# First batch of a fused attention and FFN kernel: k's first heads over a hardware queue, q in token quarters, units of scores formed as their data lands, v in three pieces

## The chip, the cores and the metric

One core of a Trainium2 chip; the runs are spread over several chips. The metric is the device time of one execution in microseconds (us). The profiled span is about 1.75 us shorter than the time of the same execution, and 1 us is 0.17% of it, so this case is about tenths of a per cent.

## The reference

Linear attention with keys and values projected from 1024 to 64 positions, then a SwiGLU FFN. Cut to what matters:

```python
# q, k, v: (8 batches, 8 heads, 1024 tokens, 64); E, F: (64, 1024)
k_proj = einsum('ks,bhsd->bhkd', E, k)
v_proj = einsum('ks,bhsd->bhkd', F, v)
scores = (q @ k_proj.transpose(0, 1, 3, 2)) / 8
attn = softmax(scores)                       # over 64 positions
x = (attn @ v_proj) -> (8192 tokens, 512)    # heads side by side
g = x @ w_gate                               # 512 x 1536
out = (silu(g) * (x @ w_val)) @ w_out
```

## The kernel before

Everything runs in bf16 on TensorE; GpSimd's loads cast fp32 to bf16 on the way. The attention of batch b+1 is woven into the FFN of batch b. Only the first batch has nothing to hide behind, and the change concerns it alone. Its work is written as units, called in the order in which TensorE runs them:

- `turn`: E or F to bf16 and token-major (fp32 transposes on TensorE, then a copy).
- `u_KV`: k or v of some heads times E or F, then casts out of PSUM (`ks` for k; `BDV` for v).
- `u_KT`: ks transposed into the block-diagonal `BD` (four copies by VectorE).
- For each of four units u of the first token half (u = 2 x head group + token pair): `u_T` transposes q, `u_S` forms scores and exp (ACT), `u_R` row sums and reciprocals (VectorE), `u_N` the product `AA` (GpSimd or VectorE), `u_A` transposes AA into `AT`.
- `u_PV2`: AT times BDV gives `xT`, which `f_mm` multiplies by the FFN's weights.
- `warm`: matmuls on zeros that keep TensorE busy. `load_w_gv(a, b)`: the columns of f = a to b-1 of w_gate and w_val.
- The first token half is 512 tokens. The first FFN groups take them as two parts of 256; where "second token half" is said of an FFN group, the second 256 are meant.

```python
# loads are issued in this order by GpSimd; E and F by SP
load_k(0, 0, 4)
... E, F ...
load_k(0, 4, 8)
load_q(0, 0, 2)            # first token half of q, as two groups of heads
load_v(0, (0, 4, 8))       # v as two halves
load_w_gv(0, 1); load_w_gv(1, 2); load_w_gv(2, 4)
warm(8); turn(0); turn(1); warm(7)
u_KV(0, "k", (0, 4), at="y")
...                        # u_KT, then k's second half, u_KT
...                        # u_T and u_S of the four units, u_R, u_N of units 0 and 2
load_w_gv(4, 6, (0,))
u_KV(0, "v", (0, 4), at="y")
...                        # A0, products of units 1 and 3, A2
u_KV(0, "v", (4, 8), at="y")
...                        # the other loads; u_PV2, A1, A3, and four half groups of f_mm
```

The softmax here doesn't subtract the row's maximum and nothing guards it: scores larger than these inputs give would overflow.

Of the kernel before, what the change touches and what calls it, by code (L numbers as in the profile page):

```python
# [12 lines left out]
BF16 = mybir.dt.bfloat16  # L13
FP32 = mybir.dt.float32

B = 8
H = 8
S = 1024
D = 64
KP = 64  # L20
DM = H * D
DFF = 1536
P = 128
NJ = S // P
# [10 lines left out]
def kernel(  # L35
# [19 lines left out]
    nc = tc.nc  # L55
# [4 lines left out]
    kv_pool = ctx.enter_context(tc.tile_pool(name="kv", bufs=2))  # L60
# [22 lines left out]
    kb, vb, qb, xT, hT = {}, {}, {}, {}, {}  # L83

    def load_k(b, h0=0, h1=H):
        if h0 == 0:
            kb[b] = kv_pool.tile([P, H, NJ, D], BF16, name="kb", tag="kb")
        nc.gpsimd.dma_start(  # L88
            out=kb[b][:, h0:h1].rearrange("p h j d -> p h (j d)"),
            in_=k[b, h0:h1].rearrange("h (p j) d -> p h (j d)", j=NJ),  # L90
        )

    def load_v(b, heads=(0, H)):
        t = kv_pool.tile([P, H, NJ, D], BF16, name="vb", tag="vb")
        vb[b] = t
        for h0, h1 in zip(heads, heads[1:]):
            nc.gpsimd.dma_start(
                out=t[:, h0:h1].rearrange("p h j d -> p h (j d)"),
                in_=v[b, h0:h1].rearrange("h (p j) d -> p h (j d)", j=NJ),
            )  # L100

    def load_q(b, ch, parts=1):
        t = q_pool.tile([P, H, 4, D], BF16, name="qb", tag="qb")
        qb[b, ch] = t
        n = H // parts
        for i in range(parts):
            nc.gpsimd.dma_start(  # L107
                out=t[:, i * n : (i + 1) * n].rearrange("p h j d -> p h (j d)"),
                in_=q[b, i * n : (i + 1) * n].rearrange("h (p c j) d -> p c h (j d)", c=2, j=4)[:, ch],
            )  # L110

    def load_w_gv(c0, c1, which=(0, 1)):
        cs = slice(c0 * P, c1 * P)
        for wsrc, wdst in [((moe_w_gate, wg), (moe_w_val, wv))[i] for i in which]:
            nc.gpsimd.dma_start(
                out=wdst[:, :, cs],
                in_=wsrc[:, cs].rearrange("(t p) c -> p t c", p=P),
            )
# [11 lines left out]
    def bank(where, shape, dt, name):  # L130
        pool, tag = banks[where]
        return pool.tile(shape, dt, name=name, tag=tag)

    def copy(eng, out, in_):
        (nc.scalar.copy if eng is nc.scalar else eng.tensor_copy)(out=out, in_=in_)  # L135
# [31 lines left out]
    def u_KT(b, at="a", prs=(0, NPAIR)):  # L167

        ks = kvp[b, "s"]
        t = bank(at, [P, NPAIR, KP], BF16, "kTp")  # L170
        for pr in range(*prs):
            nc.tensor.transpose(  # L172
                out=t[:, pr, :],
                in_=ks[:, 2 * pr : 2 * pr + 2, :].rearrange("p h d -> p (h d)"),
                identity=ident_bf[:KP, :KP],
            )
        bd = BD[b % 2][:].rearrange("p (a c) k -> p a c k", c=2)
        for c in range(2):
            src = t[64 * c : 64 * c + 64, slice(*prs)]
            nc.vector.tensor_copy(out=bd[0:64, slice(*prs), c, 0:64], in_=src)  # L180
            nc.vector.tensor_copy(out=bd[64:128, slice(*prs), c, 64:128], in_=src)
# [65 lines left out]
    def u_N(b, u):  # L247
        ch, w = divmod(u, 4)
        g, i = divmod(w, 2)
        if (b, ch) in BY_DMA:  # L250
            if (b, ch, "d") not in AA:
                AA[b, ch, "d"] = aw.tile([P, 4, H, KP], BF16, name="AAd", tag="AAd")
            a = AA[b, ch, "d"][:, 2 * i : 2 * i + 2, 4 * g : 4 * g + 4, :]
        else:
            a = AA[b, u] = aw.tile([P, 2, 4, KP], BF16, name="AA", tag="AA", bufs=4)
            a = a[:]
        eng = nc.vector if b == 0 and u in (2, 3) else nc.gpsimd
        eng.tensor_tensor(  # L258
            out=a.rearrange("p j h k -> p h j k"),
            in0=ee.pop((b, u))[:],  # L260
            in1=rr.pop((b, u))[:].unsqueeze(3).to_broadcast([P, 4, 2, KP]),
            op=ALU.mult,
        )
# [160 lines left out]
            fn(*a)  # L424

    with tc.manual_schedule():
        load_k(0, 0, 4)
        ef = []
        for which, src in (("E", E), ("F", F)):
            raw = const.tile([KP, S], FP32, name=f"{which}raw")  # L430
# [7 lines left out]
            nc.vector.memset(BD[i][:], 0.0)  # L438
            nc.vector.memset(BDV[i][:], 0.0)

        def turn(which):
            for half in range(2):
                ps = bank("v", [P, 4, KP], FP32, "efp")
                for i in range(4):
                    j = 4 * half + i
                    nc.tensor.transpose(
                        out=ps[:, i, :],
                        in_=ef[which][:, bass.ds(j, P, step=NJ)],
                        identity=ident_fp[:KP, :KP],
                    )  # L450
                js = slice(4 * half, 4 * half + 4)
                copy((nc.scalar, nc.vector)[which], (ET, FT)[which][:, js, :], ps[:])

        def warm(n):

            ps = bank("v", [P, CW], FP32, "warm")
            for _ in range(n):
                nc.tensor.matmul(
                    out=ps[:], lhsT=zeros[:, 0:P], rhs=zeros[:],
                    start=True, stop=True,  # L460
                )


        load_k(0, 4, 8)
        load_q(0, 0, 2)
        load_v(0, (0, 4, 8))
        load_w_gv(0, 1)
        load_w_gv(1, 2)
        load_w_gv(2, 4)
        warm(8)  # L470
        turn(0)
        turn(1)
        warm(7)
        u_KV(0, "k", (0, 4), at="y")
        warm(2)
        u_KT(0, at="v", prs=(0, 2))
        warm(2)
        u_KV(0, "k", (4, 8), at="y")
        warm(2)
        u_KT(0, at="v", prs=(2, 4))  # L480
        u_T(0, 0, "a", nc.scalar)
        u_T(0, 1, "a", nc.vector)
        u_T(0, 2, "a", nc.scalar)
        u_S(0, 0, "g")
        u_T(0, 3, "v", nc.vector)
        u_S(0, 2, "g")
        u_S(0, 1, "a")
        u_S(0, 3, "a")
        u_R(0, 0)
        u_N(0, 0)  # L490
        u_R(0, 2)
        u_N(0, 2)
        load_w_gv(4, 6, (0,))
        u_KV(0, "v", (0, 4), at="y")
        warm(1)
        u_A(0, 0, nc.scalar)
        u_R(0, 1)
        u_N(0, 1)
        u_R(0, 3)
        u_N(0, 3)  # L500
        u_A(0, 2, nc.scalar)
        u_KV(0, "v", (4, 8), at="y")
        load_w_gv(4, 6, (1,))
        load_q(0, 1)
        load_w_gv(6, 8)
        load_w_gv(8, 10)
        load_w_gv(10, 12)
        load_wo(0)
        load_wo(1)
        load_k(1)  # L510
        warm(1)
        u_PV2(0, 0, 0, 0, nc.scalar)
        u_PV2(0, 0, 1, 0, nc.vector)
        u_A(0, 1, nc.scalar)
        u_A(0, 3, nc.vector)
        f_mm(0, 0, 0, 0)
        f_mm(0, 0, 1, 0)
        u_PV2(0, 0, 0, 1, nc.scalar)
        u_PV2(0, 0, 1, 1, nc.vector)
        f_mm(0, 1, 0, 0)  # L520
        f_mm(0, 1, 1, 0)

# [32 lines left out]
        for t in range(NIT):  # L555
            c, f = divmod(t, NFT)
# [40 lines left out]
```

## Time and profile before

| | before |
|---|---|
| time, median of 3 | 574.07 us (573.66 to 574.24) |
| span of the profiled run | 572.4 us |
| k's first heads land; their matmuls start | 9.70; 9.74 |
| k's other heads land; their matmuls start | 12.25; 12.29 |
| v's last byte lands; v's last matmuls start | 20.01; 20.05 |
| marker: first f=0 group of the second token half | 24.88 |
| from marker to end | 547.5 |

Read it from the bottom: 547.5 us of TensorE work without a gap follow the marker, so a change to the opening can win only by moving the marker (24.88). Each step above the marker starts 0.04 us after its data lands. Windows of the profile before: after the window and its length, busy time of PE, PEld, DVE, ACT and POOL with counts; then the granted clock, a DMA figure that is not used here, and GB/s.

```profile
20.00:23.00 3.00, 2.70 (x23) 1.98 (x25) 2.53 (x6) 1.97 (x5) 2.82 (x4) 1.00 1.64 189
23.00:26.00 3.00, 3.00 (x29) 2.68 (x29) 0.89 (x2) 1.07 (x2) 2.93 (x5) 1.00 1.45 196
```

After v, the weights stream on at the same pace, 189 and 196 GB/s (the last column).

### The profile page before, as it was taken

The numbers are of one execution on the slowest core, as the hardware profiler recorded it, in microseconds if no ns is written. First come the engines' busy times: TensorE is split into PE (matmuls) and PEld (weight loads), VectorE is DVE, ScalarE is ACT, GpSimd is POOL, SyncE is SP. The second block draws the span as 40 slices with busy tenths as digits, with TensorE's granted clock in tenths as the row PEclk, the third lists the DMA queues.
The fourth block names the chain that finished last, engine by engine and source line by source line (L and its number), as shares of the span: only waits on it lengthen the run. The fifth ranks groups of instructions, "written<-read, shape, count | busy, mean of one in ns | idle before, by whom it ended". The sixth has DMA issues, their size and how long they took to land.

```text
span 572.4 us, 7867 instructions
## 1 busy us (share of the span) xinstructions
PE 561.2 (98%) x2910; PEld 268.6 (47%) x2967; DVE 336.8 (59%) x580; ACT 237.0 (41%) x416; POOL 107.9 (19%) x121
## 2 busy tenths in 40 slices
PE   8899999999999999999999999999999999999997
PEld 4654544444444444444444444444444444444444
DVE  2787566666466744766556665567546674554550
ACT  1655444353425434444335434354342543443232
POOL 6734131234002400124001330023200220000000
PEclk9999999999999999999999999999999999999999
DMA  9999993539901698037951399204990124100012
GB/s 160 196 200 206 201 161 74 93 64 196 201 37 41 110 190 157 18 75 129 187 108 38 59 179 195 63 22 88 197 176 37 42 52 74 38 37 25 31 39 92
DMA packets 105927, 61.34 MB, mean 107 GB/s; under 512 B 58016, under 2 KB 97696, under 8 KB 105888
## 3 DMA queue, kind: packets, MB, share of 16 engines
q0 software_dynamic: 42288, 29.89, 36.1%
q1 hardware_dynamic: 63312, 30.68, 25.1%
q8 instruction: 23, 0.38, 0.3%
q10 hardware_dynamic: 288, 0.26, 0.1%
q14 instruction: 16, 0.13, 0.1%
HBM read 60.29 MB, written 16.78 MB: 135 GB/s over the span
## 4 chain that ended last, share of the span: by engine, by line
PE 94%; DMA 2%; POOL 1%; ACT 1%; issue 1%; DVE 0%; POOLq 0%
PE yps L360 29%; PE vps L322 29%; PE gps L322 29%; PE kvp L147 3%; PE sc L227 2%; DMA vb<-in_v_dram 2%; PE pv L285 2%; PE aTp L274 0%; ACT xT L135 0%; PE qTp L193 0%; POOL kb L88 0%; PE kTp L172 0%; POOL qb L107 0%; ACT th L334 0%; PE pv L300 0%
## 5 line engine op out<-in xcount | busy, mean ns | idle before, releaser
L341 DVE SCALAR_TENSOR_TENSOR s<-th,gps 128x512 f32<-128x512 f32 x192 | 130.5, 680 | 138.0 <-ACT th L334 137.8
L322 PE MATMUL gps<-xT,wg 128*128 128x512 bf16 (+1 forms) x755 | 195.7, 377 | 1.2
L322 PE MATMUL vps<-xT,wv 128*128 128x512 bf16 (+1 forms) x761 | 195.9, 377 | 0.8
L360 PE MATMUL yps<-wo,hT 128*128 128x512 bf16 (+2 forms) x761 | 191.5, 376 | 0.8
L334 ACT ACTIVATE th<-gps 128x512 f32<-128x512 f32 x192 | 114.6, 597 | 162.6 <-PE gps L322 155.1
L346 DVE TENSOR_TENSOR hT<-s,vps 128x512 bf16<-128x512 f32 x192 | 132.0, 688 | 22.1 <-PE vps L322 1.5
L360 PEld LDWEIGHTS <-hT 128*128 128x128 bf16 x780 | 76.2, 98 | 89.9
L258 POOL TENSOR_TENSOR AAd<-ee,rr 128x512 bf16<-128x512 f32 x52 | 54.1, 1040 | 319.5 <-issue 168.4
L322 PEld LDWEIGHTS <-wv 128*128 128x128 bf16 x776 | 73.9, 98 | 82.9 <-issue 3.3
L322 PEld LDWEIGHTS <-wg 128*128 128x128 bf16 x776 | 74.0, 98 | 81.3 <-issue 0.6
L370 ACT ACTIVATE ysb<-yps 128x512 f32<-128x512 f32 (+1 forms) x65 | 38.4, 590 | 78.1 <-PE yps L360 74.4
L135 ACT CAST xT<-pv 128x512 bf16<-128x512 f32 x62 | 36.1, 585 | 51.3 <-PE pv L285 50.3
L242 DVE TENSOR_REDUCE zz<-ee 128x8 f32<-128x512 f32 x64 | 43.5, 679 | 17.9 <-ACT ee L231 17.9
L231 ACT ACTIVATE ee<-sc 128x512 f32<-128x512 f32 x64 | 37.9, 595 | 17.4 <-PE sc L227 17.4
L285 PE MATMUL pv<-AT,BDV 128*128 128x512 bf16 x60 | 22.6, 379 | 0.1
L227 PEld LDWEIGHTS <-qTd 128*128 128x128 bf16 x208 | 16.0, 98 | 12.3
L227 PE MATMUL sc<-BD,qTd 128*128 128x128 bf16 x208 | 20.1, 219 | 0.1
L135 DVE CAST BDV<-kvp 64x256 bf16<-64x256 f32 x14 | 6.0, 426 | 22.1 <-ACT ks L157 19.1
L258 POOL TENSOR_TENSOR AA<-ee,rr 128x512 bf16<-128x512 f32 x10 | 10.3, 1038 | 35.2 <-DVE rr L244 33.6
L147 PE MATMUL kvp<-kb,ET 128*64 128x512 bf16 (+1 forms) x72 | 15.5, 357 | 1.3 <-DMA kb<-in_k_dram 1.3
L244 DVE RECIPROCAL rr<-zz 128x8 f32<-128x8 f32 x64 | 13.0, 203 | 6.2
L147 PE MATMUL kvp<-vb,FT 128*64 128x512 bf16 (+1 forms) x72 | 15.5, 358 | 1.0 <-DMA vb<-in_v_dram 1.0
(49 smaller groups left out, 144.8 us busy)
## 6 DMA issues: line engine op xcount, KB each, us to landing
out_dram<-ysb SPq DMA_DIRECT2D x63, 256.0 KB, 2.3
qb<-in_q_dram POOLq DMA_DIRECT2D x15, 512.0 KB, 16.6
kb<-in_k_dram POOLq DMA_DIRECT2D x7, 1024.0 KB, 11.6
vb<-in_v_dram POOLq DMA_DIRECT2D x7, 1024.0 KB, 14.2
wo<-in_moe_w_out_dram POOLq DMA_DIRECT2D x2, 768.0 KB, 14.8
wg<-in_moe_w_gate_dram POOLq DMA_DIRECT2D x5, 256.0 KB, 10.4
wv<-in_moe_w_val_dram POOLq DMA_DIRECT2D x5, 256.0 KB, 10.4
kb<-in_k_dram POOLq DMA_DIRECT2D x2, 512.0 KB, 8.7
```

The source lines that it names most:

```text
L135: (nc.scalar.copy if eng is nc.scalar else eng.tensor_copy)(out=out, in_=in_)
L147: nc.tensor.matmul(out=t[lo : lo + 64, h0:h1].rearrange("p h d -> p (h d)"), lhsT=w[:, j, :], rhs=src[b][:, h0:h1, j, :], start=(j == 0), ...
L227: nc.tensor.matmul(out=ps[:, n, :], lhsT=t[:, n, :], rhs=BD[b % 2][:, 4 * g + n, :], start=True, stop=True)
L231: nc.scalar.activation(out=e[:].rearrange("p h j k -> p (h j k)"), in_=ps[:].rearrange("p a k -> p (a k)"), func=AF.Exp, scale=scale,)
L242: nc.vector.reduce_sum(out=z[:], in_=e[:], axis=AX.X)
L258: eng.tensor_tensor(out=a.rearrange("p j h k -> p h j k"), in0=ee.pop((b, u))[:], in1=rr.pop((b, u))[:].unsqueeze(3).to_broadcast([P, 4, 2 ...
L322: nc.tensor.matmul(out=ps[:, ts], lhsT=(wg, wv)[w][:, kt, f * P : (f + 1) * P], rhs=x[:, kt, ts], start=(kt == 0), stop=(kt == NKT - 1),)
L334: nc.scalar.activation(out=th[:], in_=ps[:], func=AF.Tanh, scale=0.5)
L341: nc.vector.scalar_tensor_tensor(out=s1[:], in0=th[:], scalar=1.0, in1=g[:], op0=ALU.add, op1=ALU.mult)
L346: nc.vector.tensor_tensor(out=hT[c][:, f, :], in0=s1[:], in1=ps[:], op=ALU.mult)
L360: nc.tensor.matmul(out=yy[c][:, cs], lhsT=hT[c][:, f, i * P : (i + 1) * P], rhs=wo[:, f, cs], start=(f == 0), stop=(f == NFT - 1),)
L370: nc.scalar.activation(out=ysb[:, cs], in_=yy[c][:, cs], func=AF.Copy, scale=0.5)
```

## The change

Its intent is to use the DMA engines earlier and to have less left to do when the last byte of v lands. Cut to its core (helpers for the new q slices and tile allocation are left out, as is the rest of the order; also, the copies of F leave VectorE for ACT, and the product of unit 2 leaves VectorE for GpSimd, which then has three):

```diff
-        load_k(0, 0, 4)
+        kraw = [aw.tile([P, 2, NJ * D], FP32, ...) for tag in ("qTd", "AAd")]
+        for i in range(2):
+            nc.scalar.dma_start(out=kraw[i][:], in_=k[0, 2 * i : 2 * i + 2]...)   # fp32, ACT's queue
...
+        load_q(0, 0, (0, 2))
         load_k(0, 4, 8)
-        load_q(0, 0, 2)
-        load_v(0, (0, 4, 8))
+        load_q(0, 0, (2, 4))
+        load_v(0, (0, 4, 6, 8))
         load_w_gv(0, 1)
-        load_w_gv(1, 2)
-        load_w_gv(2, 4)
+        load_w_gv(1, 2, (0,))
...
+        ... casts of kraw to kb, 3.5 heads on VectorE and half a head on ACT
         u_KV(0, "k", (0, 4), at="y")
+        ... T0, T2, scores, sums and product of unit 0
+        load_w_gv(1, 2, (1,))
+        turn(1, "a")
+        warm(1)
         u_KV(0, "k", (4, 8), at="y")
+        ... T1, A0, T3; scores, sums and products of units 2, 1
+        load_w_gv(2, 4)
+        ... unit 3
         u_KV(0, "v", (0, 4), at="y")
-        u_KV(0, "v", (4, 8), at="y")
+        u_KV(0, "v", (4, 6), at="y")
+        u_PV2(0, 0, 0, 0, act)
+        u_A(0, 2, act)
+        u_A(0, 1, act)
+        warm(1)
+        u_KV(0, "v", (6, 8), at="y")
+        u_PV2(0, 0, 1, 0, act)
+        ...
+        load_w_gv(4, 6)
```

More of the change, by code (lines that the diff above doesn't have):

```diff
@@ L85, in load_k @@
     def load_k(b, h0=0, h1=H):
-        if h0 == 0:
+        if b:
             kb[b] = kv_pool.tile([P, H, NJ, D], BF16, name="kb", tag="kb")
@@ L93, in load_v @@
     def load_v(b, heads=(0, H)):
-        t = kv_pool.tile([P, H, NJ, D], BF16, name="vb", tag="vb")
-        vb[b] = t
+        if heads[0] == 0:
+            vb[b] = kv_pool.tile([P, H, NJ, D], BF16, name="vb", tag="vb")
+        t = vb[b]
         for h0, h1 in zip(heads, heads[1:]):
@@ L100, in load_v, with load_q @@
             )
-    def load_q(b, ch, parts=1):
-        t = q_pool.tile([P, H, 4, D], BF16, name="qb", tag="qb")
-        qb[b, ch] = t
-        n = H // parts
-        for i in range(parts):
-            nc.gpsimd.dma_start(
-                out=t[:, i * n : (i + 1) * n].rearrange("p h j d -> p h (j d)"),
-                in_=q[b, i * n : (i + 1) * n].rearrange("h (p c j) d -> p c h (j d)", c=2, j=4)[:, ch],
-            )
+    def load_q(b, ch, js=(0, 4)):
+        if js[0] == 0:
+            qb[b, ch] = q_pool.tile([P, H, 4, D], BF16, name="qb", tag="qb")
+        js = slice(*js)
+        nc.gpsimd.dma_start(
+            out=qb[b, ch][:, :, js, :].rearrange("p h j d -> p h (j d)"),
+            in_=q[b].rearrange("h (p c j) d -> p c h j d", c=2, j=4)[:, ch, :, js, :].rearrange(
+                "p h j d -> p h (j d)"
+            ),
+        )
     def load_w_gv(c0, c1, which=(0, 1)):
@@ L256, in u_N @@
             a = a[:]
-        eng = nc.vector if b == 0 and u in (2, 3) else nc.gpsimd
+        eng = nc.vector if (b, u) == (0, 3) else nc.gpsimd
         eng.tensor_tensor(
@@ L426 @@
     with tc.manual_schedule():
-        load_k(0, 0, 4)
+        kb[0] = kv_pool.tile([P, H, NJ, D], BF16, name="kb", tag="kb")
+        kraw = [aw.tile([P, 2, NJ * D], FP32, name="kraw", tag=tag) for tag in ("qTd", "AAd")]
+        for i in range(2):
+            nc.scalar.dma_start(
+                out=kraw[i][:],
+                in_=k[0, 2 * i : 2 * i + 2].rearrange("h (p j) d -> p h (j d)", j=NJ),
+            )
         ef = []
@@ L439, with turn @@
             nc.vector.memset(BDV[i][:], 0.0)
-        def turn(which):
+        def turn(which, at):
             for half in range(2):
-                ps = bank("v", [P, 4, KP], FP32, "efp")
+                ps = bank(at, [P, 4, KP], FP32, "efp")
                 for i in range(4):
@@ L451, in turn @@
                 js = slice(4 * half, 4 * half + 4)
-                copy((nc.scalar, nc.vector)[which], (ET, FT)[which][:, js, :], ps[:])
+                copy(nc.scalar, (ET, FT)[which][:, js, :], ps[:])
         def warm(n):
@@ L461, in warm @@
                 )
+        dve, act = nc.vector, nc.scalar
+        load_q(0, 0, (0, 2))
         load_k(0, 4, 8)
-        load_q(0, 0, 2)
-        load_v(0, (0, 4, 8))
+        load_q(0, 0, (2, 4))
+        load_v(0, (0, 4, 6, 8))
         load_w_gv(0, 1)
-        load_w_gv(1, 2)
-        load_w_gv(2, 4)
-        warm(8)
-        turn(0)
-        turn(1)
-        warm(7)
+        load_w_gv(1, 2, (0,))
+        warm(11)
+        turn(0, "v")
+        warm(4)
+        for h in range(4):
+            for n in range(2):
+                eng = act if (h, n) == (3, 1) else dve
+                ds = slice(256 * n, 256 * (n + 1)) if h == 3 else slice(0, 512)
+                if n == 0 or h == 3:
+                    copy(eng, kb[0][:, h].rearrange("p j d -> p (j d)")[:, ds], kraw[h // 2][:, h % 2, ds])
@@ L474 @@
         u_KV(0, "k", (0, 4), at="y")
+        warm(1)
+        u_T(0, 0, "a", act)
+        u_KT(0, at="v", prs=(0, 2))
+        u_T(0, 2, "a", act)
         warm(2)
-        u_KT(0, at="v", prs=(0, 2))
-        warm(2)
-        u_KV(0, "k", (4, 8), at="y")
-        warm(2)
-        u_KT(0, at="v", prs=(2, 4))
-        u_T(0, 0, "a", nc.scalar)
-        u_T(0, 1, "a", nc.vector)
-        u_T(0, 2, "a", nc.scalar)
         u_S(0, 0, "g")
-        u_T(0, 3, "v", nc.vector)
-        u_S(0, 2, "g")
@@ L487 @@
-        u_S(0, 1, "a")
-        u_S(0, 3, "a")
         u_R(0, 0)
         u_N(0, 0)
+        load_w_gv(1, 2, (1,))
+        turn(1, "a")
+        warm(1)
+        u_KV(0, "k", (4, 8), at="y")
+        warm(1)
+        u_KT(0, at="v", prs=(2, 4))
+        warm(1)
+        u_T(0, 1, "a", act)
+        u_A(0, 0, dve)
+        u_T(0, 3, "a", dve)
+        u_S(0, 2, "g")
         u_R(0, 2)
         u_N(0, 2)
-        load_w_gv(4, 6, (0,))
+        u_S(0, 1, "g")
+        u_R(0, 1)
+        u_N(0, 1)
@@ L494 @@
+        load_w_gv(2, 4)
+        u_S(0, 3, "v")
+        u_R(0, 3)
+        u_N(0, 3)
         u_KV(0, "v", (0, 4), at="y")
         warm(1)
-        u_A(0, 0, nc.scalar)
-        u_R(0, 1)
-        u_N(0, 1)
-        u_R(0, 3)
-        u_N(0, 3)
-        u_A(0, 2, nc.scalar)
-        u_KV(0, "v", (4, 8), at="y")
-        load_w_gv(4, 6, (1,))
+        u_KV(0, "v", (4, 6), at="y")
+        u_PV2(0, 0, 0, 0, act)
+        u_A(0, 2, act)
+        u_A(0, 1, act)
+        warm(1)
+        u_KV(0, "v", (6, 8), at="y")
@@ L504 @@
+        u_PV2(0, 0, 1, 0, act)
+        u_A(0, 3, dve)
+        u_PV2(0, 0, 0, 1, dve)
+        load_w_gv(4, 6)
         load_q(0, 1)
-        load_w_gv(6, 8)
-        load_w_gv(8, 10)
-        load_w_gv(10, 12)
+        for f in (6, 8, 10):
+            load_w_gv(f, f + 2)
         load_wo(0)
@@ L510 @@
         load_k(1)
-        warm(1)
-        u_PV2(0, 0, 0, 0, nc.scalar)
-        u_PV2(0, 0, 1, 0, nc.vector)
-        u_A(0, 1, nc.scalar)
-        u_A(0, 3, nc.vector)
         f_mm(0, 0, 0, 0)
+        u_PV2(0, 0, 1, 1, act)
         f_mm(0, 0, 1, 0)
-        u_PV2(0, 0, 0, 1, nc.scalar)
-        u_PV2(0, 0, 1, 1, nc.vector)
         f_mm(0, 1, 0, 0)
```

## The prediction

> **What bounds the kernel now.** I read the page's chain of work first: it says which engine sets the end, and whether a change confined to the first batch can matter.
>
> ```profile
> span 572.4 us, 7867 instructions
> PE 561.2 (98%) x2910; PEld 268.6 (47%) x2967; DVE 336.8 (59%) x580; ACT 237.0 (41%) x416; POOL 107.9 (19%) x121
> PE 94%; DMA 2%; POOL 1%; ACT 1%; issue 1%; DVE 0%; POOLq 0%
> ```
>
> TensorE carries 94% of the chain. The waits list of TensorE from 30 us on is empty, so from there it runs without a gap and its work is fixed. The change leaves the work of that part alone. What can move is when that part begins. The rest of the chain (DMA, POOL, issue) lies in the first 21 us, so I next read TensorE in order of time there, with what ended each idle stretch.
>
> ```profile
> 5.86 1.09 PE L446 MATMUL efp<-ident_fp,Fraw 64*128 64x64 f32 x8
> 7.03 1.67 PE L458 MATMUL warm<-zeros 128*128 128x512 bf16 x7
> 9.74 1.03 PE L147 MATMUL kvp<-kb,ET 128*64 128x256 bf16 x8 [1.04 <-DMA kb<-in_k_dram]
> 12.29 1.03 PE L147 MATMUL kvp<-kb,ET 128*64 128x256 bf16 x8 [0.27 <-DMA kb<-in_k_dram]
> 17.50 1.03 PE L147 MATMUL kvp<-vb,FT 128*64 128x256 bf16 x8 [0.61 <-DMA vb<-in_v_dram]
> 20.05 1.06 PE L147 MATMUL kvp<-vb,FT 128*64 128x256 bf16 x8 [0.41 <-DMA vb<-in_v_dram]
> 22.57 0.73 PE L322 MATMUL gps<-xT,wg 128*128 128x256 bf16 x4
> 24.88 0.60 PE L322 MATMUL gps<-xT,wg 128*128 128x256 bf16 x4
> ```
>
> Each stage starts as its data lands: k's first heads at 9.7, the rest of k at 12.25, v at 17.46 and 20.01. The last chain is: v lands 20.01, 8 matmuls to 21.12, two BDV casts to 21.69, attention times v, then four half groups of the FFN (L322). The second token half of f=0 starts at 24.88; I use this as the marker. From it to the end is 572.4 - 24.88 = 547.5 us of unbroken TensorE work. The run time exceeds the profiled span by about 1.7 (574.07 against 572.4).
>
> Last, how well the start uses the DMA (windows of the opening; last three columns are clock, DMA share, GB/s at the destination; a load that casts to bf16 reads twice that):
>
> ```profile
> 0.00:2.50 2.50, 1.31 (x4) 0.48 (x5) 1.52 (x5) 1.28 (x1) 1.38 (x7) 1.00 0.11 29
> 5.00:7.50 2.50, 2.37 (x19) 1.95 (x19) 0.85 (x2) 0.74 (x2) 2.50 (x4) 1.00 1.16 163
> 7.50:8.50 1.00, 1.00 (x6) 0.35 (x4) 0.00 (x0) 0.00 (x0) 0.94 (x2) 1.00 0.83 96
> 8.50:11.00 2.50, 1.46 (x11) 0.98 (x10) 0.00 (x0) 0.19 (x1) 0.74 (x1) 1.00 1.23 198
> 14.00:17.00 3.00, 2.26 (x33) 1.85 (x33) 2.21 (x7) 2.18 (x5) 1.41 (x2) 1.00 1.24 206
> ```
>
> From 8.5 us on the loads run at about 200 GB/s (400 read); before that they do not. The steady pace is 2.55 us per MiB read (v's two halves land at 17.46 and 20.01). Five MiB of k, q, v plus 0.5 of E and F, at that pace from the first packet at 2.2 us and with 0.6 from last packet to landing, would end near 16.8 for the median engine; the trace has 18.8. So about 2.0 us of DMA time are lost before 8.5 us. One engine's share also lands about 0.9 us behind the others on every load issued by GpSimd (k's first half: 15 of 16 increments by 8.55, the last at 9.70); E and F, issued by SP, spread by only 0.65 and 0.44.
>
> **What the Trainium skill says.** "DMA: Bandwidth & Descriptors", section "SWDGE vs HWDGE vs iDMA": a cast needs the software path of GpSimd, a plain copy can take the hardware path of SP or ACT. That is why k's first heads arrive as fp32 and are cast by VectorE. Same page, "Issuing engines are not separate DMA queues": all issuers share 16 engines, only issue time is saved. So the new queue can fill idle DMA time but not raise the 400 GB/s; the trace agrees that before 8.5 us there is idle time. Same page, "Specifications": runs under 512 B are below line rate. The trace agrees: w columns in 256 B rows landed 0.73 us apart per 0.25 MiB read, against 0.64 at the steady pace, and q's token quarters now have such rows. "SBUF — State Buffer", "Who interferes with whom": a VectorE cast from SBUF to SBUF in a two-port mode locks GpSimd out. No such cast runs before, so its duration is an estimate: between half and all of the 0.69 us of the 128x512 cast from PSUM.
>
> **The change part by part.**
>
> (1) k's heads 0-3 go by ACT as two fp32 loads, issued near 0.74 and 1.3 instead of GpSimd's 1.25-2.19 plus the 1.4 us from there to its first packet. E, F and these move 1.5 MiB from 2.2 us; at 2.55 per MiB that ends at 6.0, at the poorer early pace near 7. Landing near 7-7.6, no straggler, then a cast and a half (0.5-1.0): the k matmuls start near 8.2, not 9.74. GpSimd, freed of one issue (0.94), issues the first q quarter near 2.4.
>
> (2) Stream after that. I credit 1.2 of the 2.0 lost us as recovered. Against it, two q quarters in 256 B rows cost 2 x 0.5 MiB x 0.36 us per MiB (four times 0.73-0.64) = 0.36, rounded to 0.3. Net 0.9: the last byte of v lands near 19.1 instead of 20.0. k's second half is now behind a q quarter: 12.25 + 1.3 - 1.2, near 12.4, no earlier than before. The second q quarter lands near 13.9 (before: 14.93).
>
> (3) The end of v. Two heads instead of four are left when the last piece lands: 8 matmuls of 128 columns (estimate 0.65, from 1.03 for 256 and the 98 ns of a weight load) instead of 1.06, and smaller BDV casts (0.45 for 0.54): -0.5. Of the attention-value work of the first token half, only the second group and one late copy are left after it; two aTp groups (0.76) leave that place. The four xT copies and four half FFN groups remain. Without other waits the marker would be v's landing + 0.65 + 0.45 + 0.35 + 0.6 (xT on ACT, which the third matmul of the f=0 group needs) + 4 x 0.44 + about 0.1, so 19.1 + 3.9 = 23.0.
>
> (4) The score chain, which was 1 us clear of that, gets close. The two last units need k's second half and q's second quarter. k's second half 12.4, matmuls to 13.45, ks cast 13.85, transposes 14.15, four BD copies of 0.23 to 15.1; T1 and T3 copied by 15.95; the three exps at 0.55 apart end at 16.25, 16.8, 17.3. VectorE then does three reduce-and-reciprocal pairs (0.83 each, back to back, 16.3 to 18.7) and unit 3's product (0.92) to 19.6; GpSimd does units 2 and 1 (1.04 each) from 17.2 to 19.3. TensorE's order puts unit 1's transposes ahead of v's last two heads, so that part starts at about 19.8, not 19.1. ACT is queued as well: BDV, xT, two AT copies at about 0.55 end near 20.7. That pushes the last BDV cast and the marker by 0.7: 23.7.
>
> Sum: marker between 23.0 (DMA sets it) and 23.7 (scores set it); I take 23.4, hence 24.88 - 23.4 = 1.5 us gained. Warm-up matmuls stay 23 in number and the 8 added v matmuls are small and inside waits.
>
> **Rivals.**
>
> (a) The hardware queue recovers nearly all of the 2.0 us and k's second half lands near 11.6. For it: E and F have no straggler and reached their landing 3.7 us after issue. Against: the 163 GB/s just after them, while nothing else ran. It would give a gain of 2.2 us: 571.8.
>
> (b) The scores or ACT are later still, because F's transposes and copies now sit on TensorE and ACT between the units, and three products wait in order behind one another. For it: before, VectorE is busy 2.86 of 3.00 us in 17-20. The gain shrinks to 0.5: 573.6. If the first SWDGE transfer keeps its 2 us straggler and it is now q, which unit 0 needs, that only delays unit 0, which has slack.
>
> (c) Weights become the wait. GpSimd issues w columns 2-3 only after unit 1's product (near 19), where before it was 13.9. The queue holds three weight pieces (about 2 us) at v's end, so a hole of 0.5-1 us is possible. The columns of f=6 landed at 32.30 and 33.63, used at 33.79 and 34.87: slack 1.5 and 1.2. With TensorE 1.5 earlier and DMA only 0.9 minus the hole, slack falls to between 0.9 and nothing. At worst 0.5 of the gain is given back: 573.1.
>
> (d) A half-rate clock after longer idle at 7-12 us. Every window above has a granted clock of 1.00, with idle of 1.04 us; I give it little.
>
> **Range and chances.** 574.07 - 1.5 = 572.6. The ends: all DMA time recovered and no score wait, gain 2.6, gives 571.5; scores and a weight hole together, gain 0.2, gives 573.9. 2% is 11.5 us, more than the whole of the idle time in the opening, so faster or slower by that much is practically excluded.
>
> **What would show it.** The marker (first 128x256 gps group that runs with no gap into the 128x512 ones) at 23.4 instead of 24.88, and 547.5 us after it unchanged. k's first matmuls near 8.2. v's last landing near 19.1. What ended the wait before v's last matmuls: AA of unit 1 if (4) holds, v's DMA if it does not. A wait of TensorE on wg or wv after 30 us would prove (c). I am wrong if v lands later than 19.8, if the marker moved by less than 0.4, or if the time from marker to end changed by over 0.4.

## The result, and the profile after

The changed kernel took 574.45 us (median of 4, 574.04 to 574.49); the kernel before, beside it, 574.15 (median of 4, 573.66 to 575.08). The ratio is 1.0002 (95% interval 0.9984 to 1.0019): the same within 2%. The predicted 572.6 is 1.85 us too low, and the result lies outside the range of 571.5 to 573.9.

TensorE in order of time in the changed kernel (start, busy us, engine, line, operation; in brackets the idle time before it and what ended it):

```profile
6.03 1.07 PE L455 MATMUL efp<-ident_fp,Eraw 64*128 64x64 f32 x8 [0.76 <-DMA Eraw<-in_E_dram]
8.74 1.03 PE L149 MATMUL kvp<-kb,ET 128*64 128x256 bf16 x8 [0.60 <-DVE kb L137]
11.78 1.09 PE L455 MATMUL efp<-ident_fp,Fraw 64*128 64x64 f32 x8
13.13 1.06 PE L149 MATMUL kvp<-kb,ET 128*64 128x256 bf16 x8
18.71 0.61 PE L149 MATMUL kvp<-vb,FT 128*64 128x128 bf16 x8 [0.30 <-ACT BDV L137]
20.08 0.40 PE L276 MATMUL aTp<-ident_bf,AA 128*128 128x128 bf16 x4 [0.21 <-POOL AA L260]
20.63 0.63 PE L149 MATMUL kvp<-vb,FT 128*64 128x128 bf16 x8
24.57 0.60 PE L324 MATMUL gps<-xT,wg 128*128 128x256 bf16 x4
```

k's first matmuls start 1.0 us earlier than before (8.74), but the marker moved by only 0.31, to 24.57. v's last byte lands at 18.43 in this trace; v's last matmuls start at 20.63, so 2.2 us after their data, where before it was 0.04. k's second half lands at 11.88 and its matmuls start at 13.13, because F's transposes hold TensorE from 11.78 to 12.87 and a warm-up matmul follows. And the weights: the same windows as those of before,

```profile
20.00:23.00 3.00, 2.51 (x25) 1.73 (x26) 1.16 (x3) 2.38 (x6) 3.00 (x6) 1.00 0.99 111
23.00:26.00 3.00, 3.00 (x30) 2.68 (x29) 0.60 (x2) 1.18 (x2) 3.00 (x5) 1.00 1.25 147
```

show 111 and 147 GB/s for 189 and 196. GpSimd, which issues the loads, says why (its order of time in the changed kernel):

```profile
17.99 2.04 POOL L260 TENSOR_TENSOR AA<-ee,rr 128x512 bf16<-128x512 f32 x2 [2.60 <-ACT ee L233]
19.98 0.80 POOL L117 DMA_DIRECT2D wg<-in_moe_w_gate_dram  x1
```

The issue of w's columns 2-3 stands behind the products of units 2 and 1 and comes at 19.98 (before: 13.93). Later the FFN pays for it, in the order of time of TensorE:

```profile
32.62 1.03 PE L324 MATMUL vps<-xT,wv 128*128 128x512 bf16 x4
33.77 1.04 PE L324 MATMUL gps<-xT,wg 128*128 128x512 bf16 x4
34.65 0.39 PE L195 MATMUL qTp<-ident_bf,qb 128*128 128x128 bf16 x4
35.15 1.04 PE L324 MATMUL vps<-xT,wv 128*128 128x512 bf16 x4
```

A group of four 128x512 matmuls takes 0.86 from start to start where nothing waits. Here 1.15 pass between 32.62 and 33.77: wg of f=6 lands at 33.72 (before: 32.30), wv at 35.10 (before: 33.63). These two waits, 0.3 us each, are why marker to end is 548.1 and not 547.5. They are too short for the profile's list of waits, which is empty; only the start times show them.

### The profile page after: what moved, and what is told of

Its sections match the earlier page's. It is cut to its first block, busy times and chain, and to the rows that moved or that the text cites. A ratio compares the mean times of both kernels' runs of the same rounds, so it can differ in the third digit from the quotient of the medians.

```text
span 572.7 us, 7896 instructions
## 1 busy us (share of the span) xinstructions
PE 561.8 (98%) x2919; PEld 268.8 (47%) x2975; DVE 336.2 (59%) x580; ACT 238.9 (42%) x422; POOL 109.1 (19%) x122
## 3 DMA queue, kind: packets, MB, share of 16 engines
q10 hardware_dynamic: 832, 1.31, 0.7%
## 4 chain that ended last, share of the span: by engine, by line
PE 92%; DMA 3%; DVE 2%; POOL 1%; issue 1%; ACT 1%; ACTq 0%; DVEq 0%; POOLq 0%
PE yps L362 29%; PE vps L324 27%; PE gps L324 27%; PE kvp L149 3%; PE sc L229 2%; PE pv L287 2%; DMA wv<-in_moe_w_val_dram 2%; DMA kraw<-in_k_dram 1%; DVE zz L244 1%; PE qTp L195 0%; POOL wg L117 0%; DVE hT L348 0%; PE kTp L174 0%; DVE s L343 0%; ACT xT L137 0%
## 5 line engine op out<-in xcount | busy, mean ns | idle before, releaser
L244 DVE TENSOR_REDUCE zz<-ee 128x8 f32<-128x512 f32 x64 | 43.5, 679 | 19.3 <-ACT ee L233 19.3
L137 DVE CAST BDV<-kvp 64x256 bf16<-64x256 f32 x14 | 6.0, 427 | 22.1 <-ACT ks L159 19.1
L149 PE MATMUL kvp<-vb,FT 128*64 128x512 bf16 (+2 forms) x80 | 15.7, 339 | 0.3 <-ACT BDV L137 0.3
```

Source lines behind the costliest of these rows:

```text
L137: (nc.scalar.copy if eng is nc.scalar else eng.tensor_copy)(out=out, in_=in_)
L149: nc.tensor.matmul(out=t[lo : lo + 64, h0:h1].rearrange("p h d -> p (h d)"), lhsT=w[:, j, :], rhs=src[b][:, h0:h1, j, :], start=(j == 0), ...
L244: nc.vector.reduce_sum(out=z[:], in_=e[:], axis=AX.X)
```

## The experiments

All outputs are right. Each ratio compares an experiment with runs of the kernel before on the same chip. Both kernels were also profiled again, since one profile of each may be unusual.

### Is the late issue of weights a cause? e1 takes it away, p4 puts it into the kernel before

```diff
 # e1: the changed kernel
+        load_w_gv(2, 4)        # ahead of the products of units 2 and 1
         u_N(0, 2)
...
         u_N(0, 1)
-        load_w_gv(2, 4)
```

> The changed kernel, with the two issues of weight columns 2-3 moved on GpSimd from behind units 2's and 1's products to ahead of them. Theory A (these late issues, 19.98 and 20.78 us, leave a hole in the load stream that reaches the f=6 weights and gives two TensorE waits of 0.3 us): issues near 15 and 16, 20-23 us back to about 190 GB/s from 111, f=6 weights land by 32.5 and 33.9 instead of 33.72 and 35.10, no TensorE wait there, marker (first f=0 group of the second token half) unchanged at 24.57, span 572.7 - 0.6 = 572.1. Theory B (the stream itself is slower, short 256 B rows, more bytes as fp32): landings near 33.7 and 35.1 as before, span 572.7.

Measured: the list of waits stays empty, the weights of f=6 land at 32.08 and 33.40, and the window 20 to 23 us is full again:

```profile
20.00:23.00 3.00, 2.39 (x24) 1.64 (x25) 1.15 (x3) 2.49 (x6) 3.00 (x5) 1.00 1.58 186
```

Marker 24.68, span 572.2, so marker to end is 547.5 again. Time 574.55 (573.97 to 575.99) against 573.67 of before: ratio 1.0016 (1.0003 to 1.0028).

```diff
 # p4: the kernel before
-        load_w_gv(2, 4)        # issued right behind v
...
-        load_w_gv(4, 6, (0,))
         u_KV(0, "v", (0, 4), at="y")
         ...                    # A0, product of unit 1
         u_N(0, 1)
+        load_w_gv(2, 4)
+        load_w_gv(4, 6, (0,))
```

> The kernel before, with the suspected fault put in: the issues of weight columns 2-3 and of the gate's 4-5 moved behind the second GpSimd product (near 21.2 us). Theory A (late issue makes a hole that reaches f=6): a window of low rate near 22-24 us, f=6 weights land near 34.0 and 35.3 instead of 32.30 and 33.63, TensorE waits there of 0.2 to 0.6 each, marker unchanged at 24.9, span and time up by 0.5 to 1.0. Theory B (issue order does not matter, the queue refills in time): span as before.

Measured: the gate's columns 2-3 issued at 19.78 and landed at 23.75; the two groups of f=6 start 0.66 and 0.24 us later than where nothing waits:

```profile
33.08 1.04 PE L322 MATMUL gps<-xT,wg 128*128 128x512 bf16 x4 [0.50 <-DVE s L341]
34.42 1.04 PE L322 MATMUL vps<-xT,wv 128*128 128x512 bf16 x4
```

The profile names a VectorE instruction, but wg of f=6 landed at 33.04, 0.04 before that matmul: the wait is the DMA's. Marker to end is 548.5, that is 1.0 more than the kernel before. Time 574.64 against 573.50, ratio 1.0016 (0.9998 to 1.0034). In the traces both directions agree: issuing weights behind a product costs 0.6 in the changed kernel and 1.0 here, where the marker is early. These are one trace each, and the times alone do not show it: the interval of p4 includes 1, and e1 did not run beside the changed kernel. In p4 the front of the kernel is that of before, and v landed at 18.64, 1.4 us earlier than in the first profile of before, with the marker at 23.51. That put the baseline itself in question.

### Is the baseline profile typical? r_before, and all runs of before

> The kernel before, one more profile. Theory C (the first profile of it had an unusually slow start of the load stream, k's first half landing at 9.70 and v at 20.01; the typical run is like the one of p4, 7.85 and 18.64): k's first half lands before 8.6, v near 18.6 to 19, marker near 23.5 to 24, span near 571.3. Theory D (the first profile is typical): 9.7, 20.0, 24.9, 572.4.

```profile
8.87 1.03 PE L147 MATMUL kvp<-kb,ET 128*64 128x256 bf16 x8 [0.18 <-DMA kb<-in_k_dram]
19.20 1.06 PE L147 MATMUL kvp<-vb,FT 128*64 128x256 bf16 x8 [0.42 <-DMA vb<-in_v_dram]
24.03 0.60 PE L322 MATMUL gps<-xT,wg 128*128 128x256 bf16 x4
```

The unchanged kernel, once more: everything 0.85 us earlier than in its first profile, k's first heads landing at 8.83, v at 19.16, marker 24.03, span 571.6. The first load of one and the same kernel lands earlier or later from run to run, and this moves through v to the marker. It does not start later: the first packet of GpSimd's queue is at 3.57 us in the first profile, 3.58 here and 4.32 in p4. A load reports its landing in 16 increments of a semaphore, and it is mostly the last of them that is late: 9.70, 8.83 and 7.85, where the 15th came at 8.55, 7.95 and 7.83. Over 44 runs of before on four chips the span has a median of 571.8 and goes from 570.9 to 574.3; 18 of the 44 are at 571.6 or below. The first profile (572.4) is among the slower ones.

### Do F's transposes delay the scores? e2

```diff
         u_T(0, 2, "a", act)
-        warm(2)
+        turn(1, "a")           # F, while BD is being written
         u_S(0, 0, "g")
...
-        turn(1, "a")
-        warm(1)
         u_KV(0, "k", (4, 8), at="y")
```

> The changed kernel, with F's eight transposes moved from ahead of k's second half into the wait for the BD copies of the first half (two warm matmuls and one more go). Theory A (the score chain starts late because TensorE is at F's transposes when k's second half lands at 11.88): its matmuls start near 12.2 instead of 13.13, the marker moves from 24.57 to 23.7, the weight issues behind the products move with it, span near 571.9. Theory B (what holds v's last heads is ACT's queue at 19.8 to 21.8, not the chain's start): marker 24.3 or later, span 572.5.

```profile
12.50 1.06 PE L149 MATMUL kvp<-kb,ET 128*64 128x256 bf16 x8
15.42 0.40 PE L276 MATMUL aTp<-ident_bf,AA 128*128 128x128 bf16 x4 [0.62 <-POOL AA L260]
16.67 0.40 PE L229 MATMUL sc<-BD,qT 128*128 128x128 bf16 x4 [0.18 <-DVE qT L137]
24.54 0.60 PE L324 MATMUL gps<-xT,wg 128*128 128x256 bf16 x4
```

k's second half started 0.63 earlier, and then TensorE stood for 0.62 before unit 0's transposes of AA, which come two groups later in its order and need GpSimd's product. The last scores came at 16.67 for 16.70 and the marker at 24.54 for 24.57. Time 574.76 against 573.67, ratio 1.0025 (1.0005 to 1.0045). The expected marker failed: the wait moved one instruction group on.

### Does v's end stand behind unit 1? e3

```diff
         u_PV2(0, 0, 0, 0, act)
+        u_KV(0, "v", (6, 8), at="y")   # ahead of A2 and A1
         u_A(0, 2, act)
         u_A(0, 1, act)
         warm(1)
-        u_KV(0, "v", (6, 8), at="y")
```

> The changed kernel, with the matmuls of v's last two heads and their casts put ahead of the transposes of units 2 and 1 on TensorE and ACT; weights as in the changed kernel. Theory A: v's last matmuls start near 19.85 (after the cast of the piece before, same bank) instead of 20.63, the marker moves to about 23.8; but the f=6 weights still land at 33.7 and 35.1, so the waits on them grow from 0.6 to about 1.4 in sum and the span stays at 572.7 within 0.2. Theory B (weights are not a bound): span falls by the 0.8 too, to 571.9.

```profile
20.21 0.61 PE L149 MATMUL kvp<-vb,FT 128*64 128x128 bf16 x8 [0.19 <-ACT BDV L137]
21.94 0.38 PE L302 MATMUL pv<-AT,BDV 128*128 128x256 bf16 x2 [0.36 <-ACT AT L137]
24.74 0.60 PE L324 MATMUL gps<-xT,wg 128*128 128x256 bf16 x4
```

v's end ran at 20.21 (in a run whose k matmuls were 0.36 later, at 13.49), and what was won there was waited for at 21.94, for ACT's copy of AT. Marker 24.74, time 575.08 against 573.67, ratio 1.0021 (1.0010 to 1.0033). The expected marker of 23.8 failed; ACT's queue was the next wait.

### All three together, and a redone order: e5, e6

e5 holds the edits of e1, e2 and e3. e6 goes further:

```diff
 # e6, against the changed kernel
+        load_w_gv(1, 2); load_w_gv(2, 4) both ahead of unit 1's product
+        turn(1, "a") while BD is being written; u_A(0, 0) after the last scores
-        u_KV(0, "v", (4, 6), at="y")
+        u_KV(0, "v", (4, 6), at="g")     # v's middle piece in a PSUM bank of its own
-        u_A(0, 1, act), u_A(0, 3, dve), u_PV2(0, 0, 0, 1, dve) ahead of f_mm
+        u_A(0, 1, dve), u_A(0, 3, act), u_PV2(0, 0, 0, 1, dve) among the f_mm of f=0 and f=1
```

> All three edits together. Theory A: marker near 23.0 to 23.4, f=6 weights near 32.3 and 33.7, waits of at most 0.6 on them, span near 571.6, time near 573.3, about 0.8 below the kernel before. If the hole comes from the bandwidth and not from the issue order: waits of 1.5 to 2 on the weights and span 572.7.

> The changed loads with the compute order redone: weight columns 1-3 issued ahead of the products, F's transposes in the first BD wait, unit 0's transposes behind the last scores, v's middle piece in a PSUM bank of its own, and units 1 and 3 (needed only by the second token half) between the FFN groups of the first half. If the loads now bound everything: first FFN group near 20.3, marker near 22.7 to 23.2, waits on wg or wv of up to 0.5 in sum, span near 570.6, time 1.5 to 2 below the changed kernel. If something else still binds the opening: marker above 23.8 and span above 571.5.

e5: marker 24.40 (its expected 23.0 to 23.4 failed), no waits, span 571.9, 573.68 against 573.67, ratio 1.0002 (0.9990 to 1.0015). e6: marker 23.88, no waits, span 571.5, 573.65 against 573.50, ratio 1.0003 (0.9984 to 1.0021). So with its waits taken out one by one the changed loading order reaches the kernel before, and no more. Against the changed kernel that is a gain: on e6's chip the four later runs of the changed kernel at clock 1.0 took 574.43 to 575.41, e6's five 573.31 to 574.68. In e6 v's last matmuls began at 18.87, 0.25 after v landed, and the first FFN group stood for 0.45 on ACT's xT.

### The changed kernel again, and the clock: r_after

> The changed kernel once more, so that it stands on one chip beside the other kernels of this call and beside the kernel before. Expected as in its first profile: marker near 24.6, load rate near 110 GB/s in 20-23 us, two TensorE waits near 33.8 and 35.1 of 0.3 each; time equal to the kernel before within 0.2%, if anything above it. If the first profile was an accident of one chip, the marker or the waits differ.

Its profiled run showed something else. These are its windows; the clock is the third number from the right:

```profile
5.00:8.00 3.00, 1.69 (x11) 1.28 (x11) 0.57 (x2) 0.74 (x2) 3.00 (x5) 0.88 1.12 246
8.00:11.00 3.00, 2.42 (x10) 1.20 (x8) 0.63 (x2) 0.40 (x1) 0.85 (x2) 0.50 1.62 191
11.00:14.00 3.00, 3.00 (x17) 1.57 (x16) 0.89 (x4) 1.46 (x3) 0.13 (x1) 0.50 1.53 194
```

TensorE had been idle for 1.31 us in one piece, from 5.03 to 6.34, waiting for E, and at 7.25 the clock halved: k's first matmuls took 1.86 instead of 1.03, the marker came at 27.19, the span was 575.5 at a mean clock of 0.994. The other four runs, at 1.0, had spans of 572.7 to 573.6. Median 574.91 against 573.50, ratio 1.0023 (1.0002 to 1.0043). The halved clock is thus a loss of some runs, not the reason for the typical 574.5. The length of a gap does not decide it alone: the profile of u1 below has a gap of the same 1.31 us and the first one of before a gap of 1.04, both at full clock.

### One part alone: p1 (k by ACT in the kernel before) and u1 (the changed kernel without it)

```diff
 # p1: the kernel before
-        load_k(0, 0, 4)
+        kraw = ...             # two fp32 loads by ACT
...
         warm(7)
+        ...                    # the casts of kraw
         u_KV(0, "k", (0, 4), at="y")
```

> The kernel before, with one part of the change alone: k's first four heads by ACT as fp32 with casts; q in head halves, v in two halves, weight issues and compute order as before. Theory A (the earlier stream is a real gain that the compute order around it then gives away): v lands near 18.5 to 19.0 instead of 20.01, weights follow early (f=6 at 31 and 32.3), no wait there, marker about 0.8 to 1.2 earlier than 24.88, span near 571.4. Theory B (the stream is no faster, its gain in the changed kernel came from elsewhere): v near 20, span 572.4.

```profile
8.53 1.12 PE L452 MATMUL efp<-ident_fp,Fraw 64*128 64x64 f32 x8 [1.53 <-ACT kb L135]
12.48 1.06 PE L147 MATMUL kvp<-kb,ET 128*64 128x256 bf16 x8
26.42 0.60 PE L322 MATMUL gps<-xT,wg 128*128 128x256 bf16 x4
```

576.11 against 573.50, ratio 1.0048 (1.0029 to 1.0067): part 1 alone is harmful, which neither theory had expected. k's raw data landed at 8.09, but E and F, which share the DMA engines with it, came at 5.79 and 8.39 (first profile of before: 4.45 and 5.66). F's transposes stand ahead of k's matmuls in TensorE's order, the seven warm-up matmuls between them ran at the halved clock (2.84 us, before 1.67; clock 0.62 in 8 to 11 us), and k's matmuls began at 12.48. The halved clock is not all of the loss: the one run at 1.0 had a span of 574.3. The profile puts the 1.53 wait down to a cast by ACT; that F landed at 8.39, 0.14 before, points to F as well. The changed kernel escapes this by moving F's transposes back, and that is what put them in front of k's second half.

```diff
 # u1: the changed kernel
-        kraw = ... and its casts
+        load_k(0, 0, 4)        # by GpSimd, as before
```

> The changed kernel with its first part undone: k's first four heads again by GpSimd as bf16, no fp32 load and no casts; everything else as in the changed kernel. Theory C (the hardware path for k gains nothing against a typical start, because E and F then queue behind it): E lands near 4.5 and F near 5.8 instead of 5.9 and 8.5, k's first half near 8, its matmuls near 8.6, v's last piece at 18.5 to 19.2, marker 24.2 to 25, time within 0.6 us of the changed kernel. Theory D (it recovers 1 us or more, as predicted): v's last piece and the marker 1 us later than in the changed kernel, time up by 1.

```profile
9.48 1.03 PE L149 MATMUL kvp<-kb,ET 128*64 128x256 bf16 x8 [1.31 <-DMA kb<-in_k_dram]
25.58 0.60 PE L324 MATMUL gps<-xT,wg 128*128 128x256 bf16 x4
```

In this profile everything from k's second half on is 1.0 later than in the changed kernel's first (v landed at 20.01), span 573.6; but of its six runs three had spans of 571.5 to 572.1, while the changed kernel's (not run beside it) were 572.2 to 573.6 at full clock. Median 574.59 against 573.59, ratio 1.0022 (1.0003 to 1.0041). So part 1 shows no gain over these runs. What it does change is the spread of the start: in the eleven profiles with k by ACT in the changed kernel's order v's last byte lands between 18.43 and 18.90 (mean 18.60), in the four with k by GpSimd between 18.64 and 20.01. It is again one share: the 15th of v's last 16 increments comes at 18.34 to 18.86 in the eleven and at 18.52 to 19.15 in the four, but the 16th follows within 0.24 in the eleven, and 0.12 to 1.08 later in the four.

### Is it the three pieces of v? u3

```diff
-        load_v(0, (0, 4, 6, 8))
+        load_v(0, (0, 4, 8))
-        u_KV(0, "v", (4, 6), at="y")
...
-        u_KV(0, "v", (6, 8), at="y")
+        u_KV(0, "v", (4, 8), at="y")
```

> The changed kernel with v in two halves again, as before; all else as changed. Theory A (v's third piece is not what its matmuls wait for: they come behind unit 1's transposes at 20.6, two microseconds after v has landed): the last v matmuls start at 20.6 or slightly earlier, take 1.05 instead of 0.6, casts 0.54 for 0.43; marker and time up by 0 to 0.5. Theory B (the short end is worth the 0.5 predicted and more because v is the wait): up by 0.6 or more, with the wait before v's last matmuls ended by v's DMA.

Measured: 575.07 against 573.59, ratio 1.0032 (1.0020 to 1.0044), but two of the five runs had the low clock (0.997). The three at 1.0 had spans of 572.9 to 573.3, against 572.7 to 573.6 for four runs of the changed kernel on another chip: no difference that I can claim. In its profile, one of the two with the low clock, v's last matmuls, which came at 22.26, waited for A1 (0.61 idle on GpSimd's product) and not for v, landed at 18.55. A short last piece is worth little where the last piece is not what is waited for.

### Towards a better version: e7, w1, e8

e7 is e6 with v's last casts on VectorE, all four products on GpSimd, and the copy of A2 ahead of xT on ACT; beyond what its expectation says, one warm-up matmul is gone and the transposes of units 1 and 3 come one FFN group earlier.

> The redone kernel (e6) with the end of the score chain spread over the engines: the last v casts on VectorE, all products on GpSimd, unit 2's copy ahead of the first xT copy on ACT. If ACT's queue held e6 at 23.88: last v casts near 19.5 instead of 20.28, first FFN group near 20, marker near 23.2, span near 570.9, time 0.6 below e6 and 0.5 below the kernel before. If the loads hold it: waits on wg or wv at 21 to 23 or at 32 to 33, span unchanged at 571.5.

Measured: three runs at clock 1.0 with spans of 570.8, 570.9 and 571.2, and two at 0.997 with 572.4 and 572.7. Median 572.97 against 573.59, ratio 0.9995 (0.9982 to 1.0008). Its profile is of a run with the low clock, so the expected marker of 23.2 was not seen. Last, the clock: w1 adds warm-up matmuls to the changed kernel, e8 to e7.

```diff
 # w1: the changed kernel
-        warm(11)
+        warm(14)
         turn(0, "v")
-        warm(4)
+        warm(8)
 # e8: e7 with only the second of these
```

> The changed kernel with 7 more warm-up matmuls: 3 before E's transposes, 4 before k's first matmuls. If idle TensorE makes the half-rate clock: no run with a mean granted clock below 0.998, all windows of the profile up to 14 us at 1.00, and none of the 2 to 3 us late runs; fast runs with a span of 572.3 to 573.2 like the changed kernel's good ones, so a ratio to before of 1.000 to 1.001 and a marker of 24.4 to 24.9. Rival: the low clock is the chip's own and comes at random; then 1 or 2 of 6 runs still show 0.997 or less and a span of 574 or more.

> The best version so far (e7_tail) with 4 more warm-up matmuls before k's first matmuls, where it had TensorE idle for 0.9 us in the profile with the low clock. If idle makes the low clock: every run with a span of 570.7 to 571.3 (as the three good ones of e7_tail), median time 572.4 to 573.0, ratio to before 0.998 to 0.999, and no run at a clock of 0.997. Rival (random): 2 of 5 runs at 0.997 with a span over 572.3 again, ratio 0.9995.

w1: all six runs at 0.999 or 1.0, so no halved clock; but the added matmuls themselves cost time. E's transposes began at 7.27 and k's first matmuls at 10.20 (8.74 in the changed kernel), the profiled marker at 26.05. Time 574.93 against 573.08, ratio 1.0026 (1.0012 to 1.0039), no better than without. The clock part of the expectation came true, that of the marker did not.

e8: five runs, all at 0.999 or 1.0, spans 570.9 to 571.3, time 572.80 (572.70 to 573.07) against 573.08 (572.69 to 574.39, 11 runs), ratio 0.9989 (0.9977 to 1.0002).

```profile
9.47 1.03 PE L149 MATMUL kvp<-kb,ET 128*64 128x256 bf16 x8 [0.53 <-DVE kb L137]
23.73 0.78 PE L323 MATMUL gps<-xT,wg 128*128 128x256 bf16 x4
```

Neither run shows that the warm-up matmuls did it: on this chip the 11 runs of before had no low clock either, while on the other three chips 8 of its 33 were at 0.997 or less. The median of e8 is the lowest of all, but the interval includes 1. Six of the 11 runs of before beside it had spans of 570.9 to 571.3 too; the other five 572.0 to 572.6. What e8 seems to gain is that the second kind is absent, not that its best is better. Whether that is so, five runs cannot settle.

## Why the prediction was wrong

That the time would stay the same within 2% was right and nearly certain, since all idle time of the opening together is smaller. The time was 1.85 us too low. Step by step:

**Step 1, k's first heads, "near 8.2": right in direction, 0.5 too early.** They land at 8.04 and the matmuls start at 8.74, after a cast of 128x512 (0.43; estimated: between 0.35 and 0.69) and one of 128x256 (0.29) on VectorE. "Landing near 7-7.6" was too hopeful: E and F and k share the engines, and E (5.90) and F (8.54) were pushed back by 1.5 and 2.9 us. The step never said what the delay of E and F would do. p1 shows what it does where the order is not adapted: +2.6 us.

**Step 2, v's last byte "near 19.1": it came earlier, at 18.43, but this was not where it counted.** The gain of 1.6 us against the first profile of before is partly the baseline's: r_before has 19.16 and p4, with the same front, 18.64. The mean of the three is 19.27, that of the eleven profiles with the changed loads 18.60, so the typical gain is 0.7 (predicted, net: 0.9), and most of the rest of the 1.6 was the late landing in one profile. Of the 0.7, only 0.25 is in the 15 shares that land first (mean of the 15th: 18.76, with the changed loads 18.51); the rest is the late 16th share, which is gone. The prediction had counted "no straggler" for k alone, and had credited 1.2 of the "2.0 us of DMA time" lost before 8.5 us as recovered: little of that came back. Rival (a) was nearer on the loads (k's second half landed at 11.88, it said 11.6), but its gain of 2.2 did not come.

**Step 3, the short end of v: as costed, without effect.** The 8 matmuls of 128 columns took 0.63 (predicted 0.65). From the start of v's last matmuls to the marker took 24.57 - 20.63 = 3.94 us, which is the predicted 3.9. But that path started late.

**Step 4, the score chain: the mechanism was right, the term was mis-sized.** The prediction had v's last heads at "about 19.8, not 19.1", behind unit 1's transposes; they started at 20.63, behind unit 1's transposes and 2.2 us after their data. The step that failed is "k's second half 12.4, matmuls to 13.45": it let the matmuls start when the data lands. The data landed even earlier, at 11.88, but F's transposes, written ahead of them, ran until 12.87, so the matmuls started at 13.13. From there the chain ran as costed: the exps ended at 17.85 (17.3), GpSimd's products of units 2 and 1 at 20.03 (19.3). e2 shows that moving F's transposes alone does not bring the 0.7 back, as unit 0's product then holds TensorE for 0.62; e3 shows the same for v's end and ACT. So three waits of similar length lie side by side, and an estimate that follows one of them finds the others behind it. Rival (b) named this, with 573.6. That F's transposes begin the delay is read from the trace; no run that moves them alone shortens the time.

**Choosing 23.4 between 23.0 and 23.7.** The two limits do not average: the later of them sets the marker. That choice was 0.3 of the error.

**Rival (c), the weights, was real and was left out of the number.** It predicted "at worst 0.5"; the two waits measured 0.3 each. e1 takes them out, p4 puts 1.0 into the kernel before.

Two of the prediction's three signs of being wrong came: the marker moved by less than 0.4 (0.31), and the time from marker to end changed by over 0.4 (0.6). The sum, against the prediction's own 572.6: 0.3 for the choice, 0.87 for the score chain (24.57 - 23.7), 0.6 for the weights; 1.77 of the 1.85. This sum is the accounting of one trace. Over more runs the picture shifts by the baseline: the changed kernel's later runs were at 1.0023 (1.0002 to 1.0043) of before's, so it is if anything slower by about a microsecond, and the first comparison, with before at 574.15, flattered it.

**Rival (d), the half-rate clock, "I give it little": it exists.** One of five runs of r_after had it (mean clock 0.994), and four of five of p1 (0.994 to 0.997); so did 8 of the 44 of before (0.996 to 0.997). It is not in the profile that the result was read from. "Every window above has a granted clock of 1.00" was read too far: in the first profile of before the clock records begin at 5.25 us, and ahead of them the view prints 1.00, although eight warm-up matmuls from 1.19 take 3.59 us and seven from 7.03 only 1.67.

On the shared engines the runs agree with the Trainium skill, but for the late share, which issue time does not explain. "DMA: Bandwidth & Descriptors", section "Issuing engines are not separate DMA queues", says that issuing from several engines saves only issue time; here k's first heads by ACT's queue land at 8.04 to 9.16 in twelve profiles, by GpSimd at 7.85 to 9.70 in four, and what the queue gained at the very start (its first half, two heads, lands at 4.5) was taken from E and F. The lockout between VectorE's casts and GpSimd, which the prediction cited, may be in the trace, though no run takes it apart: the cast of k's second head (4.86 to 5.47) ran while GpSimd issued v's first load and took 0.61 us, and one of the same shape at 8.06, with GpSimd idle, 0.43; all eleven profiles have 0.61 or 0.62 against 0.43. It ends long before the cast that k's matmuls wait for, so it cost nothing here. q's token quarters were not tried alone.

What stays open: why one share of GpSimd's first load lands up to 1.3 us behind the 15 others in some runs (only the profiled runs have a trace, so its link to the two groups of spans of before is argued, not shown), what halves the clock, and whether the steadier times of e8 come from k's hardware load.

## What to carry to other kernels

In an opening where loads, transposes, ACT, VectorE and GpSimd are each almost busy, take the engine orders into the estimate: a step starts at the later of its data and of what stands ahead of it on its engine, and the later of two limits counts, not their mean. Do not let the engine that issues loads wait on a late product ahead of an issue; an issue that came 6 us later here left a hole behind v that came back as two waits of 0.3 us in the FFN, 14 us on. And profile the baseline more than once before counting its idle time as recoverable: here the spread of the opening (1.4 us in when v lands) was as large as the gain sought.

## What the Trainium skill lacked or had wrong

- "TensorE: Matmul & The Clock Gate", sections "What's actually happening" and "Why this matters for your kernels": they put the fall to half rate after an idle window of about 3.4 us and advise against gaps of about 3 us. Here the clock fell to 0.50 after a longest single gap of 1.31 us, in a window of 3 us in which TensorE was busy for 1.69 (r_after), and the mean clock to 0.67 and 0.68 in 8 to 11 us after single gaps of 0.93 and 1.00 (e7, u3). Yet a gap of 1.31 in u1 and one of 1.04 in before did no harm. So the length of a single gap was no guide here. In their clock records the half rate lasts 3.41 us in e7, u3 and p1 and 6.83 in r_after, which fits the length of the page's window, and the page's own remark that the window runs freely fits the fact that only some runs of a kernel are hit. In all four the 3.41 us before the fall hold transposes of E; whether these count as work for the clock was not tested, and no run gives a threshold.
- "DMA: Bandwidth & Descriptors", section "Anatomy of one DMA — SWDGE (gpsimd) path": its fit, 2.0 us plus bytes at 436 GB/s, gives an estimated 3.2 us for 0.5 MiB. A load of w's columns (0.5 MiB read) issued by GpSimd when the load before it had landed took 3.92 us from the start of its issue to its landing (u3, 21.61 to 25.53; the one before landed at 21.49), of which the issue instruction is 0.80, so the fit is right only from the end of the issue.
- The same page, no section: how much the landing of a kernel's first load varies from run to run, and how far one of its 16 shares can lie behind the others. k's first heads by GpSimd landed at 7.85, 8.83 and 9.70 in three profiles of the same front (15 shares by 7.83, 7.95 and 8.55), and v at 18.64, 19.16 and 20.01.
- The same page, section "Issuing engines are not separate DMA queues": it says that loads interleave, but has no figure for what a large load on one hardware queue does to small ones issued on another at the same time. E landed at 5.79 to 6.20 and F at 8.39 to 9.24 beside k's load by ACT, against 4.39 to 4.55 and 5.66 to 5.77 without it.
- "PSUM — Partial Sum Buffer", section "Summary: rules for kernel authors": it says to target another bank while one is read, with no price. In the changed kernel v's second piece waited 0.30 us for the casts of the first, which lies in the same bank; in e6, with a bank of its own, no such wait is in the trace.
